# Sinkhorn attention with a gated MLP: q transposed by DMA, head loads begun earlier, natural token order, new order of units

## The chip, the cores and the metric

The kernel runs on one core of a Trainium2 chip. The metric is the device time of one execution in microseconds (us). The kernel before took 166.08 us (median of 3 runs, 165.85 to 168.16). A run more than 1.5% above the fastest of its kernel is called slow.

PE is the matmul engine and PEld its weight loads; DVE, ACT and POOL are the vector, scalar and general engines; SP issues most of the transfers (DMA). PSUM is the memory that matmuls write. A hole is idle time of PE, a landing is the time from the issue of a transfer to its arrival, and the granted clock is the share of PE's full clock that it was given in a stretch (1.00 is full, 0.50 is half).

## The reference, cut to what matters

```python
# q, k, v: [4 batches, 8 heads, 768 tokens, 64]; sort_net: [4, 8, 8, 8]
P = sinkhorn(sort_net)                      # 5 rounds of exp, row and column division
k_sorted = einsum('bhij,bhjcd->bhicd', P, k_blocks)    # 8 blocks of 96 tokens are mixed
v_sorted = einsum('bhij,bhjcd->bhicd', P, v_blocks)
attn = softmax(q_blocks @ k_sorted.T / 8)   # inside each block
x = (attn @ v_sorted), heads side by side   # [4, 768, 512]

h = relu(x @ w_in); u, v = halves of h      # [4, 768, 512] each
v_n = (v - mean) / sqrt(var + 1e-6)
v_s = einsum('ts,bsd->btd', w_spatial, v_n) + b_spatial
out = (u * v_s) @ w_out
```

## The kernel before

One batch is attention, then gated MLP. The program is software-pipelined: while the MLP of batch b runs, attention of batch b+1 is woven into it by a hand-written list of units. A unit is one letter (k: mix and transpose k; q: transpose q; v: mix v; s: score; a: attend; d: divide; V, N, U, S, O: the MLP), an index, a batch, the engine that empties PSUM (A or D), and a PSUM tile (0 to 3).

```python
def load_heads(x, b, name):                       # fp32 in DRAM -> bf16, 768 KB
    t = ld.tile([128, H, G * D], BF16, ...)       # two buffers of each of q, k, v
    nc.gpsimd.dma_start(out=t, in_=...)           # issued from POOL's queue

def vmix(self, hp, eng, ps):                      # mixed v -> vm, then by way of DRAM to vb
    ...
        nc.sync.dma_start(out=vd, in_=self.vm[:, half]...)      # SP's queue
        nc.sync.dma_start(out=self.vb[:, :, half]..., in_=vd...)

def qtr(self, n, eng, ps):                        # 24 transposes on PE, one copy out of PSUM
    for x in range(2):
        for g in range(G):
            for hh in range(2):
                nc.tensor.transpose(t[...], q_in[self.b][...], ident_bf)
    copy(eng, qT, t[:, :, 0:S])

def divide(self, n, eng, ps):                     # xt = acc * exp(-ln(sum))
    nc.vector.tensor_mul(
        out=self.xt[hp].rearrange("p (g i t) -> p i g t", ...)[:, i0:i0 + NB // 2],
        in0=t[:, 0, 0:HW].rearrange("p (i g t) -> p i g t", ...),
        in1=lns.rearrange("p (i g t) -> p i g t", ...))

# in the loop over the list, at the first spatial unit of batch b:
if not gmlp[b].gt and b + 2 < B:                  # the gate
    for x in range(2):
        nc.gpsimd.tensor_copy(out=gate[:, x:x + 1], in_=attn[b + 1].vb[0:1, 0, x, 0, 0:1])
    v_in[b + 2] = load_heads(v, b + 2, "v_in")    # and q_in, k_in
# ... cut ...
```

The gate is two one-element copies on POOL. They read vb, so POOL issues the loads of batch b+2 only after both halves of vb of batch b+1 have landed.

The softmax here doesn't subtract the row's maximum and nothing guards it: scores larger than these inputs give would overflow.

## Time and profile before

| | before |
|---|---|
| median of the runs | 166.11 us |
| profiled run | 169.51 us (slow), span 167.7 us |
| PE / ACT / DVE / POOL busy | 91% / 66% / 58% / 26% |
| mean granted PE clock | 0.968 |
| stage of batch 2, first v projection to the next | 37.8 us |
| stage of batch 3 | 33.7 us |

The prediction below shows the page, the stretches and the PE holes. One view that it only tells is POOL's timeline of the kernel before, around the gate in the stage of batch 2. The columns are start, length, engine, line and instruction, and in brackets the idle time before it and what ended it.

```profile
81.03 0.18 POOL L537 COPY gate<-vb 1x1 bf16<-1x1 bf16 x1 [18.67 <-DMA vb<-vd]
85.78 0.18 POOL L537 COPY gate<-vb 1x1 bf16<-1x1 bf16 x1 [4.57 <-DMA vb<-vd]
86.30 0.94 POOL L93 DMA_DIRECT2D v_in<-in_v_dram  x1 [0.35 <-issue]
...
88.99 4.86 POOL L455 TENSOR_TENSOR gt<-vs,u_sb 128x768 bf16<-128x768 f32 x3
```

POOL stands at the gate until vb has landed, then issues loads, and three multiplications of the MLP have queued up behind.

### The profile page before, as it was taken

Reading aid. Unit: us, or ns where it says so; the run is one execution under the profiler, and the core shown is the slowest. Engines: PE = TensorE matmul, PEld = TensorE weight load, DVE = VectorE, ACT = ScalarE, POOL = GpSimd, SP = SyncE. Lnnn points to the kernel's source line nnn. Section 1 sums busy time; section 2 is a strip of 40 time slices with the busy share of each in tenths; the row PEclk is TensorE's granted clock in tenths of the full one; section 3 lists DMA queues with packets and bytes.
Section 4 is the critical chain, followed back from the end, with each engine's and each line's share of the span. In section 5 each row is a group of like instructions: output and inputs, shape, how many; then the busy total and the mean of one; then the engine's idle time right before and its main releaser. Section 6 shows DMA issues by size and latency. Waiting matters only on the chain.

```text
span 167.7 us, 3907 instructions
## 1 busy us (share of the span) xinstructions
PE 151.9 (91%) x1636; PEld 88.6 (53%) x1645; DVE 97.4 (58%) x203; ACT 110.0 (66%) x181; POOL 43.1 (26%) x46
## 2 busy tenths in 40 slices
PE   0989986999999999999994999999999999999780
PEld 0266853556855544457662454457665544556330
DVE  4667887158971562389222265789232658849951
ACT  3167997459877777689954586489959974560041
POOL 7931000970029550000049330000063300000000
PEclk9999997599999999999999699999999999999999
DMA  2999999999647997604329993605400036000045
GB/s 15 197 204 209 232 257 187 205 203 236 217 110 96 203 204 193 250 33 151 129 72 160 204 195 131 250 31 178 151 23 0 4 131 250 0 0 4 0 182 193
DMA packets 21554, 23.86 MB, mean 142 GB/s; under 512 B 736, under 2 KB 18144, under 8 KB 21408
## 3 DMA queue, kind: packets, MB, share of 16 engines
q0 software_dynamic: 13760, 12.58, 46.8%
q1 hardware_dynamic: 7776, 11.02, 18.3%
q8 instruction: 13, 0.21, 0.5%
q14 instruction: 5, 0.04, 0.1%
HBM read 27.14 MB, written 8.65 MB: 213 GB/s over the span
## 4 chain that ended last, share of the span: by engine, by line
PE 62%; DVE 11%; ACT 10%; DMA 6%; issue 6%; POOL 2%; DVEq 0%; POOLq 0%; SPq 0%; ACTq 0%
PE ps L393 13%; PE ps L443 13%; PE ps L465 10%; PE ps L428 9%; PE ps L352 4%; ACT ex L338 3%; DVE vs L454 3%; PE ps L331 3%; DMA vb<-vd 3%; PE ps L359 2%; DVE gt L455 2%; PE ps L288 2%; PE ps L246 2%; PE ps L276 2%; PE ps L212 2%
## 5 line engine op out<-in xcount | busy, mean ns | idle before, releaser
L443 PE MATMUL ps<-wspT,v_sb 128*128 128x384 bf16 x192 | 34.6, 334 | 0.0
L338 ACT ACTIVATE ex<-ps 96x768 bf16<-96x768 f32 x32 | 24.3, 806 | 8.4 <-PE ps L331 8.3
L454 DVE TENSOR_TENSOR vs<-ps,b_bc 128x768 f32<-128x768 f32 (+1 forms) x20 | 15.9, 794 | 23.7 <-PE ps L443 18.8
L375 DVE TENSOR_TENSOR xt<-ps,lns 128x384 bf16<-128x384 f32 x32 | 16.9, 554 | 19.9 <-ACT lns L371 19.9
L455 POOL TENSOR_TENSOR gt<-vs,u_sb 128x768 bf16<-128x768 f32 x12 | 19.7, 1651 | 34.1 <-ACT ex L338 31.3
L443 PEld LDWEIGHTS <-v_sb 128*128 128x128 bf16 x192 | 18.2, 100 | 12.6 <-issue 1.6
L393 PE MATMUL ps<-w_in_sb,xt 128*128 128x512 bf16 x94 | 24.1, 406 | 0.3 <-DVE xt L375 0.2
L465 PE MATMUL ps<-w_out_sb,gt 128*128 128x512 bf16 x90 | 21.9, 380 | 1.1 <-DVE gt L455 0.8
L407 DVE BATCH_NORM_STATS2 stats<-v_sb 128x6 f32<-128x512 bf16 x24 | 16.3, 677 | 11.0 <-ACT v_sb L227 10.9
L428 PE MATMUL ps<-xt,w_in_sb 128*128 128x384 bf16 x128 | 22.6, 326 | 0.0
L227 ACT ACTIVATE v_sb<-ps 128x1024 bf16<-128x1024 f32 (+1 forms) x15 | 12.5, 852 | 15.5 <-PE ps L393 15.5
L365 ACT ACTIVATE lns<-ps 128x384 f32<-128x384 f32 x32 | 14.5, 486 | 3.9 <-PE ps L359 3.8
L428 PEld LDWEIGHTS <-w_in_sb 128*128 128x128 bf16 x128 | 12.2, 98 | 8.1
L221 ACT COPY o_sb<-ps 128x256 f32<-128x256 f32 (+1 forms) x11 | 7.3, 663 | 13.8 <-DVE o_sb L223 12.1
L393 PEld LDWEIGHTS <-xt 128*128 128x128 bf16 x96 | 9.9, 104 | 12.1 <-issue 2.1
L371 ACT ACTIVATE lns<-lns 128x384 f32<-128x384 f32 x32 | 15.7, 525 | 0.2
L465 PEld LDWEIGHTS <-gt 128*128 128x128 bf16 x96 | 8.6, 98 | 12.4 <-DVE gt L455 1.3
L352 PE MATMUL ps<-ex,vb 96*64 96x96 bf16 x256 | 11.4, 210 | 3.4 <-DVE vs L454 2.5
L352 PEld LDWEIGHTS <-vb 96*64 96x64 bf16 x256 | 8.7, 109 | 8.5 <-issue 7.1
L227 ACT ACTIVATE u_sb<-ps 128x768 bf16<-128x768 f32 x13 | 10.3, 808 | 1.7 <-PE ps L428 1.2
L359 PE MATMUL ps<-ex,ones 96*64 96x384 bf16 x64 | 11.1, 332 | 0.0
L221 ACT CAST kT<-ps 128x768 bf16<-128x768 f32 x13 | 10.0, 806 | 1.1 <-PE ps L288 1.1
(73 smaller groups left out, 177.8 us busy)
## 6 DMA issues: line engine op xcount, KB each, us to landing
out_dram<-o_sb SPq DMA_DIRECT2D x9, 512.0 KB, 2.8
q_in<-in_q_dram POOLq DMA_DIRECT2D x4, 768.0 KB, 10.4
k_in<-in_k_dram POOLq DMA_DIRECT2D x4, 768.0 KB, 13.4
v_in<-in_v_dram POOLq DMA_DIRECT2D x4, 768.0 KB, 9.7
vd<-vm SPq DMA_DIRECT2D x6, 384.0 KB, 3.7
vb<-vd SPq DMA_DIRECT2D x6, 384.0 KB, 3.9
out_dram<-o_sb SPq DMA_DIRECT2D x6, 256.0 KB, 2.1
wsp_nat<-in_moe_w_spatial_dram POOLq DMA_DIRECT2D x1, 1152.0 KB, 21.9
```

Of the source, the lines that this page charges most:

```text
L221: nc.scalar.copy(out=out, in_=in_)
L227: nc.scalar.activation(out=out, in_=in_, func=AF.Relu)
L338: nc.scalar.activation(out=e.rearrange("p h i c -> p h (i c)"), in_=t[0:BLK, :, 0:NB // 2 * BLK], func=AF.Exp, scale=scale,)
L352: nc.tensor.matmul(t[hh * 64:hh * 64 + 64, 0, ii * BLK:(ii + 1) * BLK], lhsT=self.vb[:, i, h // (H // 2), h % (H // 2), :], rhs=self.e[n][ ...
L375: nc.vector.tensor_mul(out=self.xt[hp].rearrange("p (g i t) -> p i g t", g=G, i=NB)[:, i0:i0 + NB // 2], in0=t[:, 0, 0:HW].rearrange("p (i ...
L393: nc.tensor.matmul(t[:, x, :], lhsT=self.xt[kc][:, g * 128:(g + 1) * 128], rhs=w_in_sb[:, kc, DH:DFF], start=(kc == 0), stop=(kc == KC - 1),)
L407: nc.vector.bn_stats(out=stats, in_=v_sb[:, x, :])
L428: nc.tensor.matmul(t[:, x, 0:HW], lhsT=w_in_sb[:, kc, mc * 128:(mc + 1) * 128], rhs=self.xt[kc][:, x * HW:(x + 1) * HW], start=(kc == 0), ...
L443: nc.tensor.matmul(t[:, x, 0:HW], lhsT=self.v[g][:, mc * 128:(mc + 1) * 128], rhs=wspT[:, g, x * HW:(x + 1) * HW], start=(g == 0), stop=(g ...
L454: nc.vector.tensor_add(out=vs[:, x], in0=t[:, x, 0:HW], in1=b2[:, x])
L455: eng.tensor_mul(out=gt2[:, x], in0=vs[:, x], in1=u2[:, x])
L465: nc.tensor.matmul(t[:, x, :], lhsT=self.gt[mc][:, g * 128:(g + 1) * 128], rhs=w_out_sb[:, mc, :], start=(mc == 0), stop=(mc == FC - 1),)
```

## The change

The intent: take the q transposes of batches 1 to 3 off PE (which is full), issue the loads earlier so that POOL is not held at the gate, and let the first v projection start before the last divides. The core of the diff:

```diff
-    wsp_nat ... moe_w_spatial.rearrange("(p g) s -> p g s", g=G)
+    wsp_nat ... moe_w_spatial.rearrange("(g p) s -> p g s", p=128)      # natural token order
...
+        def qdma(self, n, eng, ps):
+            qr = qr_pool.tile([128, G, H, D], BF16, name="qr", tag="qr")
+            nc.vector.tensor_copy(out=qr..., in_=q_in[self.b]...)
+            nc.sync.dma_start(out=self.q_tile(), in_=qr..., transpose=True)
...
+            if self.b == 0:          # attend of batch 0: extra matmuls for the PE clock
+                for _ in range(2):
+                    for hh in range(2):
+                        nc.tensor.matmul(t[hh * 64:hh * 64 + 64, 1, HW:512], lhsT=ones, ...)
...
-                out=self.xt[hp].rearrange("p (g i t) -> p i g t", ...)[:, i0:i0 + NB // 2],
-                in0=t[:, 0, 0:HW].rearrange("p (i g t) -> p i g t", ...),
+                out=self.xt[hp][:, ih * HW:(ih + 1) * HW].rearrange("p (i t g) -> p i t g", ...),
+                in0=t[:, 0, 0:HW].rearrange("p (i g t) -> p i t g", ...),   # and in1 alike
...
+        load_batch(2)                # before the list of units begins
...
                 if b not in gmlp:
                     gmlp[b] = Gmlp(b)
+                    if 0 < b < B - 2:
+                        load_batch(b + 2)
-                    if not gmlp[b].gt and b + 2 < B:
-                        gate = ...   # gate and loads behind it: gone
-                    eng = DVE if b == B - 1 else nc.gpsimd
+                    eng = DVE if b == B - 1 and len(gmlp[b].gt) == FC - 1 else nc.gpsimd
```

Cut: the shorter way from p to the mixing matrices, the order of the first loads, buffer counts, the whole new list of units.

## The prediction

> **What bounds the kernel now.** I read the page first (engine shares, slices, chain), then the busy table by stretches, the timeline of PE with its idle notes, the waits, the landings of the first loads, and the timelines of ACT, DVE and POOL.
>
> ```profile
> PE 151.9 (91%) x1636; PEld 88.6 (53%) x1645; DVE 97.4 (58%) x203; ACT 110.0 (66%) x181; POOL 43.1 (26%) x46
> ...
> PEclk9999997599999999999999699999999999999999
> ...
> PE 62%; DVE 11%; ACT 10%; DMA 6%; issue 6%; POOL 2%; DVEq 0%; POOLq 0%; SPq 0%; ACTq 0%
> ```
>
> PE is busy 91% and is 62% of the chain that ended last, but the clock row has two dips, one after 25 us and one after 92 us. By stretches (us, busy per engine, granted clock):
>
> ```profile
> 13.20:28.10 14.90, 12.79 (x282) 9.61 (x281) 11.66 (x18) 14.30 (x27) 0.20 (x1) 0.97 1.12 224
> 28.10:46.50 18.40, 18.18 (x195) 11.65 (x196) 11.76 (x23) 11.82 (x17) 7.48 (x4) 0.84 1.13 213
> 46.50:67.00 20.50, 20.42 (x219) 11.15 (x218) 9.71 (x19) 15.64 (x27) 9.90 (x9) 1.00 0.93 162
> 67.00:104.80 37.80, 35.16 (x375) 20.24 (x376) 17.70 (x34) 27.61 (x43) 9.55 (x9) 0.95 0.66 147
> 104.80:138.50 33.70, 33.57 (x375) 19.48 (x376) 19.06 (x35) 26.38 (x42) 6.56 (x4) 1.00 0.27 96
> ```
>
> After window and length the columns are PE, PEld, DVE, ACT, POOL, clock, DMA share and GB/s. Batch 0's attention (13.2 to 28.1) is bound by ACT, 14.3 of 14.9 us. From 28 us PE is full, so PE work taken out there comes off one for one. The stretches from 67.0 and from 104.8 hold the same work (375 matmuls each), but the first is 4.1 us longer. Finer stretches show the lost clock:
>
> ```profile
> 24.00:28.00 4.00, 2.18 (x45) 1.19 (x39) 2.72 (x7) 4.00 (x11) 0.00 (x0) 0.91 1.02 199
> 28.00:32.00 4.00, 3.78 (x13) 1.67 (x14) 1.07 (x3) 0.40 (x2) 2.84 (x2) 0.50 1.30 202
> 32.00:36.00 4.00, 4.00 (x27) 2.43 (x25) 1.64 (x4) 2.79 (x4) 4.00 (x3) 0.73 1.32 204
> ...
> 92.00:96.00 4.00, 4.00 (x34) 2.17 (x28) 1.02 (x2) 2.49 (x5) 1.85 (x2) 0.57 1.32 204
> ```
>
> Lost clock is 4 x (1 - granted): 0.36 + 2.0 + 1.08 = **3.4 us** around 24 to 36, and 1.7 us at 92. PE's timeline has these lines:
>
> ```profile
> 91.72 0.36 PE L352 MATMUL ps<-ex,vb 96*64 96x96 bf16 x8 [2.46 <-DVE vs L454]
> 115.47 0.84 PE L276 MATMUL ps<-ident_bf,q_in 128*64 128x128 bf16 x24
> 158.75 4.06 PE L465 MATMUL ps<-w_out_sb,gt 128*128 128x512 bf16 x18 [0.81 <-DVE gt L455]
> ```
>
> The first is a hole of 2.46 us. POOL's timeline explains it: POOL waited at the gate copies until both halves of vb had landed (85.78), issued three loads (86.3 to 89.0), and only then multiplied three gated tiles (4.86 us), so the PSUM tiles behind them came free late. Hole and cold clock (2.46 + 1.7) are the 4.1 us above. The profiled run took 169.51 us and is marked slow; the median is 166.08. So I count the hole in a fast run as much smaller. The second line is a q transpose unit; the third the wait in the tail.
>
> **What the Trainium skill says.** "TensorE: Matmul & The Clock Gate", Part 1: the PE clock is half or full, and about one idle window of 3.4 us drops it to half. The trace agrees: 0.50 granted from 28 to 32, after a stretch with PE busy only 2.18 of 4 us. "VectorE: DVE Perf Modes", The three transpose paths: a 128x128 bf16 transpose takes 390 ns on TensorE and 1309 ns by DMA. In this trace 24 half-width ones take 0.67 us on the chain, 28 ns each when pipelined. "DMA: Bandwidth & Descriptors", Latency and other measured facts: a DMA transpose moves an effective 261 GB/s; no run here shows one. "VectorE: DVE Perf Modes", the perf-mode tier table: a bf16 SBUF copy of 2048 elements takes 693 ns; the trace before has no such copy.
>
> **The change part by part.**
> q by DMA: removes 6 units of 24 transposes, 6 x 0.67 = 4.0 us of PE, 1.34 a batch, all on PE-bound stretches. It also removes their PSUM copies (1444 ns on ACT or 957 ns on DVE), and adds three DVE copies of 3072 elements, about 1 us each by the skill's table (an estimate), and three transposes of 768 KB. At 261 GB/s one takes 786 KB / 261 = 3.0 us plus about 2 us fixed: 5 us. At 1309 ns a block, one after the other, 24 x 1.309 = 31 us. They are issued some 15 to 20 us before the first score, so the first is hidden and the second is not.
>
> Start: transpose and spread of p go from PE-copy-PE-copy to two DVE transposes and one group of matmuls, and pdiag reads PSUM. Between p_bf (11.22) and the first k matmul (13.21) this saves about 0.3 us.
>
> Stage 0 to 1: in natural order the first three token groups need only the even units of attention, so V00 need not wait for the last divides. V now starts at 28.13; with one ACT kT copy less (0.8 us) and two units of slack I put it at 26.8. Extra matmuls in batch 0's attends (column pairs run together: 32 small ones, 16 x 55 ns = 0.9 us in ACT-bound time) and vmix units moved there should hold the clock; that is worth up to the 3.4 us. PE alone then needs, up to the first k unit, three V (5.2), three U (3.9), v11 (0.33) and five w (1.7): 37.9. But the loads were moved too. Before (issue on POOL plus time to landing, from the views of each tile), w_in landed at 21.9, wsp at 28.7, v1 at 32.6, k1 at 36.5, q1 at 40.3, so a head tile takes 3.9 us and wsp 5.5. In the new order: v1 25.8, q1 29.6, wsp 35.1, k1 39.0. So the w units wait about 1.3 us and k starts near 39.4. Adding four k (1.36), w40 (0.33), four scores (0.98) and U10 (1.3), S starts at 43.4. Before, S started at 47.26 with U30 (1.41) and a score (0.25) undone, thus 48.9. Gain **5.5 us**; without waits for loads it would be 7.
>
> Stages 2 and 3: 2 x 1.34 = **2.7 us**. Gate removed and loads issued earlier: I choose **0.7 us** for a fast run.
>
> Tail: now each of four units makes DVE do two adds and two multiplies, 2 x (0.55 + 0.56) = 2.2 us or 8.7 in all, against 2.06 of PE; PE then waits 0.81 us. Afterwards three multiplies go to POOL (1.65 us each, inside the 2 us rhythm) and only the last is split: **0.9 us**.
>
> The strided reads of the divide and the 2 KB instead of 4 KB output rows I count as zero. Sum: 5.5 + 2.7 + 0.7 + 0.9 = 9.8, so 156.3; I give back 1.2 us for new small waits of the new order: **157.5 us**.
>
> **Rivals.** (1) The DMA transpose is slow, or holds up the vd and vb transfers behind it on the same SP queue, and scores or attends wait. For it: the page's 1309 ns per block. Against it: the lead of most of a stage and low DMA load later (share 0.27 to 0.66). At 31 us each of three stages would wait 10 us or more: 185 us or worse. If only vb comes late, 1 to 3 us once: 159 to 160. (2) The clock still drops at the start of stage 1, since batch 0 stays ACT-bound and PE has gaps: then 2 to 3 us are not gained, 160. (3) Loads become the bound in stage 1: the 1.5 us already taken off, perhaps 1.5 more, 159. (4) The hole near 92 was in the median runs too: then 2 to 3 us more are gained, 155.
>
> **Range and chances.** With rival 2 plus a late vb about 162, with rival 4 and all steps right about 153.5. The limit of 2% is 162.8. Faster 0.88, same 0.09, slower 0.03 (the slow transpose).
>
> **What would show it.** No PE transposes of q in batches 1 to 3, and PE's total about 3 us less. Clock of 0.9 or more from 24 to 36. First V matmul before 27.5 and first S near 43.4, with waits for wsp or k_in in front of w or k. A landing time under 15 us for the transpose, and no score that waits for it. No gate and no PE hole of over 1 us in the third stage; the stages of batches 2 and 3 near 32.4 us. No gap before the last output projection. The prediction is wrong if PE shows waits on qT or vb, or if a stretch other than the first load waits stays under 95% PE.

## The result, and the profile after

The changed kernel took **192.25 us** (191.2 to 194.28, 4 runs). It is slower by a factor of 1.157 (95% interval 1.151 to 1.163). A ratio here is the mean time of one kernel's fast runs over that of the other's fast runs of the same rounds, so it is not quite the ratio of the medians. The predicted range was 153.5 to 162.

The page of the changed kernel answers to the first lines of the prediction:

```profile
PE 152.7 (79%) x1529; PEld 86.2 (45%) x1529; DVE 108.1 (56%) x203; ACT 101.0 (52%) x169; POOL 46.9 (24%) x44
...
PEclk9999999999555756999997579999999999999999
...
PE 46%; DMA 39%; DVE 5%; POOL 4%; issue 2%; ACT 2%; POOLq 1%; DVEq 0%
DMA qT<-qr 22%; PE ps L482 13%; PE ps L504 11%; DMA k_in<-in_k_dram 11%; PE ps L466 7%; PE ps L431 6%; DMA vd<-vm 4%; PE ps L361 3%; DVE vs L493 3%; PE ps L389 2%; DMA vb<-vd 2%; PE ps L396 2%; DVE xt L411 2%; POOL v_in L93 1%; POOLq L596 1%
```

DMA's share of the chain that ended last has gone from 6% to 39%, with the transpose of q alone at 22%. The clock row has two long dips. PE's timeline of the changed kernel has these holes:

```profile
43.35 1.20 PE L318 MATMUL ps<-pdiag,k_in 128*64 128x128 bf16 x36 [2.97 <-DMA k_in<-in_k_dram]
...
55.86 0.88 PE L361 MATMUL ps<-qT,kT 64*96 64x96 bf16 x16 [10.41 <-DMA qT<-qr]
...
69.26 0.53 PE L389 MATMUL ps<-ex,vb 96*64 96x96 bf16 x8 [6.08 <-DMA vb<-vd]
...
107.20 0.88 PE L361 MATMUL ps<-qT,kT 64*96 64x96 bf16 x16 [6.62 <-DMA qT<-qr]
```

2.97 + 10.41 + 6.08 + 6.62 = 26.1 us of PE standing still, all behind a DMA. The busy table of the changed kernel shows what follows a hole (after window and length: PE, PEld, DVE, ACT, POOL, granted clock, DMA share, GB/s):

```profile
45.50:55.90 10.40, 0.04 (x2) 0.04 (x3) 2.98 (x8) 0.33 (x2) 0.00 (x0) 0.64 1.31 183
55.90:60.00 4.10, 4.10 (x40) 2.38 (x40) 0.55 (x1) 1.56 (x3) 0.00 (x0) 0.50 1.28 225
```

PE works again from 55.9 us, at half clock. Summing length times (1 - clock) over the working stretches after the three long holes (55.9 to 64, 69.3 to 80, 107.2 to 116) gives 9.2 us. Holes and half clock are 35.3 us. In the profile of the kernel before the same items were 7.6 us (2.46 of hole, 1.7 and 3.4 of half clock). The difference is 27.7; less the 3 us or so of PE work that the change takes away (4.0 of transposes, less 0.9 of extra matmuls) this is about the 24.8 us between the spans (192.5 and 167.7).

SP's timeline of the changed kernel shows what the queue did:

```profile
30.80 14.80 SPq L310 DMA_TRANSPOSE qT<-qr  x1
45.66 0.57 SPq L275 DMA_DIRECT2D vd<-vm  x1
...
90.06 13.20 SPq L310 DMA_TRANSPOSE qT<-qr  x1
...
126.93 3.66 SPq L310 DMA_TRANSPOSE qT<-qr  x1
```

One instruction, three times: it held the SP queue for 14.80, 13.20 and 3.66 us, and landed after 25.0, 17.0 and 5.5 us. The first ran beside the rest of the first loads and the loads of batch 2, the second beside the loads of batch 3 (issued from 83.9 to 86.6 us on POOL), the third beside no load. The first vd, whose source was ready earlier, could be issued only at 45.66 us.

And the divide, one line each from the views of tile xt of the kernel before, of the changed kernel, and of the experiment a4 below (min/median/max in ns):

```profile
L375 DVE TENSOR_TENSOR xt<-ps,lns x32: 544/557/559, 22.5 to 137.4; 128x384 bf16<-128x384 f32 x32
```

```profile
L411 DVE TENSOR_TENSOR xt<-ps,lns x32: 792/806/827, 21.8 to 163.2; 128x384 bf16<-128x384 f32 x32
```

```profile
L411 DVE TENSOR_TENSOR xt<-ps,lns x32: 1427/1472/1622, 21.9 to 154.0; 128x384 bf16<-128x384 f32 x32
```

### The profile page after: what moved, and what is told of

The parts are those of the page before. It is cut to its first block, busy times and chain, and to the rows that moved or that the text cites. A ratio compares the mean times of both kernels' runs of the same rounds, so it can differ in the third digit from the quotient of the medians.

```text
span 192.5 us, 3673 instructions
## 1 busy us (share of the span) xinstructions
PE 152.7 (79%) x1529; PEld 86.2 (45%) x1529; DVE 108.1 (56%) x203; ACT 101.0 (52%) x169; POOL 46.9 (24%) x44
## 2 busy tenths in 40 slices
DMA packets 32657, 26.20 MB, mean 136 GB/s; under 512 B 10048, under 2 KB 28224, under 8 KB 32640
## 3 DMA queue, kind: packets, MB, share of 16 engines
q0 software_dynamic: 14400, 12.58, 42.4%
## 4 chain that ended last, share of the span: by engine, by line
PE 46%; DMA 39%; DVE 5%; POOL 4%; issue 2%; ACT 2%; POOLq 1%; DVEq 0%
DMA qT<-qr 22%; PE ps L482 13%; PE ps L504 11%; DMA k_in<-in_k_dram 11%; PE ps L466 7%; PE ps L431 6%; DMA vd<-vm 4%; PE ps L361 3%; DVE vs L493 3%; PE ps L389 2%; DMA vb<-vd 2%; PE ps L396 2%; DVE xt L411 2%; POOL v_in L93 1%; POOLq L596 1%
## 5 line engine op out<-in xcount | busy, mean ns | idle before, releaser
L494 POOL TENSOR_TENSOR gt<-vs,u_sb 128x768 bf16<-128x768 f32 x15 | 24.7, 1645 | 128.7 <-DVE vs L493 99.0
L482 PE MATMUL ps<-wspT,v_sb 128*128 128x384 bf16 x192 | 36.7, 350 | 0.0
L411 DVE TENSOR_TENSOR xt<-ps,lns 128x384 bf16<-128x384 f32 x32 | 24.7, 806 | 18.1 <-ACT lns L408 18.1
L493 DVE TENSOR_TENSOR vs<-ps,b_bc 128x768 f32<-128x768 f32 (+1 forms) x17 | 15.5, 910 | 29.4 <-PE ps L482 29.4
L361 PE MATMUL ps<-qT,kT 64*96 64x96 bf16 x256 | 11.8, 234 | 18.1 <-DMA qT<-qr 17.0
L482 PEld LDWEIGHTS <-v_sb 128*128 128x128 bf16 x192 | 19.1, 104 | 14.4 <-issue 3.9
L466 PE MATMUL ps<-xt,w_in_sb 128*128 128x384 bf16 x128 | 25.5, 351 | 0.0
L431 PE MATMUL ps<-w_in_sb,xt 128*128 128x512 bf16 x96 | 22.0, 379 | 0.2 <-DVE xt L411 0.2
L361 PEld LDWEIGHTS <-kT 64*96 64x96 bf16 x256 | 9.1, 142 | 24.1 <-issue 12.1
L239 ACT ACTIVATE v_sb<-ps 128x1024 bf16<-128x1024 f32 (+1 forms) x15 | 12.5, 852 | 12.5 <-PE ps L431 12.5
L235 DVE CAST kT<-ps 128x768 bf16<-128x768 f32 x12 | 11.2, 949 | 6.8 <-PE ps L318 6.7
L233 ACT COPY o_sb<-ps 128x256 f32<-128x256 f32 (+1 forms) x10 | 6.3, 629 | 15.6 <-DVE o_sb L235 11.8
L431 PEld LDWEIGHTS <-xt 128*128 128x128 bf16 x96 | 9.4, 98 | 11.2 <-issue 0.5
## 6 DMA issues: line engine op xcount, KB each, us to landing
q_in<-in_q_dram POOLq DMA_DIRECT2D x4, 768.0 KB, 18.8
k_in<-in_k_dram POOLq DMA_DIRECT2D x4, 768.0 KB, 26.8
```

The costliest lines, as they stand in the source:

```text
L361: nc.tensor.matmul(t[0:BLK, hh, ii * BLK:(ii + 1) * BLK], lhsT=self.k[hp][rows, i * BLK:(i + 1) * BLK], rhs=self.q[rows, hp, i], start=Tru ...
L411: nc.vector.tensor_mul(out=self.xt[hp][:, ih * HW:(ih + 1) * HW].rearrange("p (i t g) -> p i t g", t=TB, g=G,), in0=t[:, 0, 0:HW].rearrang ...
L431: nc.tensor.matmul(t[:, x, :], lhsT=self.xt[kc][:, g * 128:(g + 1) * 128], rhs=w_in_sb[:, kc, DH:DFF], start=(kc == 0), stop=(kc == KC - 1),)
L466: nc.tensor.matmul(t[:, x, 0:HW], lhsT=w_in_sb[:, kc, mc * 128:(mc + 1) * 128], rhs=self.xt[kc][:, x * HW:(x + 1) * HW], start=(kc == 0), ...
L482: nc.tensor.matmul(t[:, x, 0:HW], lhsT=self.v[g][:, mc * 128:(mc + 1) * 128], rhs=wspT[:, g, x * HW:(x + 1) * HW], start=(g == 0), stop=(g ...
L493: nc.vector.tensor_add(out=vs[:, x], in0=t[:, x, 0:HW], in1=b2[:, x])
```

## The experiments

Two theories. **A**: the DMA transpose is slow and everything else follows. **B**: transfers that run at the same time slow each other, and the early head loads are the root: they slow the transpose, and vd and vb as well. Rivals for parts: the SP queue order, the strided divide, the new order of units. All 15 runs gave the right output. The a-series ran on one chip, the c-series on another, the d- and e-series on a third; ratios are to runs of the kernel before. The medians below are of all runs, slow ones too.

| run | what it is | median us | ratio to before |
|---|---|---|---|
| changed | | 192.25 | 1.157 |
| a1_q_pe | changed, q on PE | 176.98 | 1.055 |
| a2_gate | changed, loads behind the landed transpose | 192.17 | 1.148 |
| a3_vq | changed, vd and vb on POOL's queue | 204.21 | 1.213 |
| a4_q_pe_div | a1, divide reads in order, writes strided | 185.33 | 1.104 |
| c1_vbgate | changed, loads behind vb | 172.50 | 1.034 |
| c2_q_pe_vbgate | a1, loads behind vb | 167.45 | 1.002 |
| c3_perm | c2, token order of before | 167.43 | 0.995 |
| c4_q23_dma | c3, q of batches 2, 3 by DMA | 164.41 | 0.972 |
| d2_wout_late | c4, output weights loaded behind vb | 161.18 | 0.970 |
| d1_nofill | d2, no extra matmuls in attend | 160.31 | 0.965 |
| d3_before_q23 | before, q of batches 2, 3 by DMA | 167.81 | 1.010 |
| d4_nat | d2, natural token order | 162.95 | 0.981 |
| e1_load3_early | d1, loads of batch 3 early | 171.53 | 1.030 |
| e3_best_q_pe | d1, all q on PE | 164.37 | 0.991 |
| e2_before_again | before | 167.45 | 1.005 |

### a1_q_pe: q on PE again

```diff
-  ... a70-1 d70-- q01A- v01A3 ...          (and q02, q03)
+  ... k31A0 r01D1 k01D3 r11D2 k21A0 ...    (r: the unit qtr of before; banks shifted)
```

> The changed kernel with one part undone: q of batches 1 to 3 transposed on PE again (six units of 24 transposes put back, PSUM banks shifted, all else kept). Theory 'the DMA transpose is the loss': the two holes before the scores (10.4 and 6.6 us), the hole before attend that waits for vb (6.1) and about 9 us of half clock after them go, 4.0 us of PE comes back: about 160 to 162 us. Rival 'the new order, the early loads or the strided divide cost it': stays above 172 us, with holes of other causes.

Measured 176.98 us, a miss: 15 us came back, not 31. The PE timeline of a1 has a new largest hole, and the chain of a1 tells its cause:

```profile
57.39 0.53 PE L389 MATMUL ps<-ex,vb 96*64 96x96 bf16 x8 [7.80 <-DMA vb<-vd]
```

```profile
37.03 11.29 DMA vd<-vm
48.34 9.00 DMA vb<-vd
```

With no transpose anywhere, vd took 11.29 us and vb 9.00 us in the stage of batch 1. In the kernel before, the longest were 4.7 and 4.6 us. What runs beside them are the loads of batch 2, issued from 20.4 to 27.1 us, and the rest of the first loads: c4 below, where the loads of batch 2 are held, still has 9.3 and 8.5 us at most. Theory A alone is dead.

### a2_gate: loads behind the landed transpose

```diff
-        load_batch(2)
+                if name == "q" and b in (1, 2):
+                    nc.gpsimd.tensor_copy(out=gate[:, 0:1], in_=attn[b].qT[0:1, 0, 0:1])
+                    load_batch(b + 1)
```

> The changed kernel, but the loads of batch b+2 are issued only after the DMA transpose of q of batch b+1 has landed (a one-element copy on POOL reads the transposed tile). Theory 'the transpose is slow only beside head loads': the second transpose lands in about 5.5 us instead of 17 and its hole of 6.6 us goes; the first still runs beside the rest of the first loads, lands in about 15 us instead of 25; total 172 to 178. Rival 'the transpose is slow by itself, and the fast third one is an exception': landing times stay 25 and 17 and the total stays near 192.

The transposes did land sooner, after 16.0, 5.9 and 5.5 us. Yet the total did not move: 192.17 us, where 172 to 178 was expected, a miss. PE's timeline of a2 shows where the time went:

```profile
65.98 0.53 PE L389 MATMUL ps<-ex,vb 96*64 96x96 bf16 x8 [9.40 <-DMA vb<-vd]
...
111.92 0.53 PE L389 MATMUL ps<-ex,vb 96*64 96x96 bf16 x8 [7.60 <-DMA vb<-vd]
```

The loads now fell onto vd and vb, whose longest landings were 12.1 us each; in front of the first scores 4.38 us of waiting for the transpose was left. One wait was traded for the other, which is what theory B says and theory A does not.

### a3_vq: vd and vb on another queue

```diff
-                nc.sync.dma_start(out=vd, ...)        # and vb
+                nc.gpsimd.dma_start(out=vd, ...)      # and vb
```

> The changed kernel with the transfers vd and vb issued from POOL's queue instead of SP's, so that they need not wait for the issue of the transpose. Theory 'the queue order holds vb back': first vd issued near 34 us instead of 45.7, the hole of 6.1 us before attend of batch 1 goes, total 6 to 9 us less, about 184. Rival 'the DMA engines are full and vb comes late from any queue': hole stays, total within 2 us of 192.

204.21 us, worse by 12, and the hole before attend of batch 1 grew to 11.52 us. The view of tile vd of a3 says:

```profile
DMA to landing us min/median/max: 2.7/4.8/30.1
```

A vd now landed 30.1 us after its issue. POOL's queue also carries the head loads, and vd came behind them. So this run does not tell how much of the 6.1 us hole was SP's queue order. It shows only that sharing a queue with the loads is worse than sharing one with the transpose.

### a4_q_pe_div: the other side of the stride

```diff
-   out= ... "p (i t g) -> p i t g",  in0, in1 = ... "p (i g t) -> p i t g"   # reads strided
+   out= ... "p (i t g) -> p i g t",  in0, in1 = ... "p (i g t) -> p i g t"   # write strided
```

> As a1_q_pe, but the divide reads PSUM and the logs in order and writes its bf16 output with a stride of 12 bytes, instead of reading both fp32 inputs with a stride of 64 bytes. Theory 'the strided fp32 reads cost 806 instead of 554 ns': the divide is back near 554 ns, DVE busy falls by about 8 us, the first V matmul starts 1 to 2 us earlier, total 2 to 3 us under a1_q_pe. Rival 'any stride costs it, or DVE is off the path': 800 ns again, or the total within 0.5 us of a1_q_pe.

The opposite: 1472 ns a divide, as shown above, and 185.33 us, 8.3 us over a1. Natural order needs a stride on one side, and reading fp32 at 64 bytes (804 ns in a1) is far cheaper than writing bf16 at 12 bytes (1472 ns). In the order of the kernel before neither is needed: it reads and writes runs of 16 tokens.

### c1_vbgate and c2_q_pe_vbgate: the gate of the kernel before

```diff
-        load_batch(2)
-                    if 0 < b < B - 2:
-                        load_batch(b + 2)
+                    if not gmlp[b].gt and b + 2 < B:       # at the first spatial unit
+                        ... two copies of attn[b + 1].vb on POOL ...
+                        load_batch(b + 2)
```

> The changed kernel with one part undone: the loads of batch b+2 are held, as in the kernel before, until both halves of vb of batch b+1 have landed (two one-element copies on POOL at the first spatial unit). q stays by DMA. Theory 'transfers slow each other: early loads delay the transpose, vd and vb': second transpose lands in about 5.5 us, its hole (6.6) and half clock go; vb of batch 1 comes some 4 us after its issue; the first transpose still runs beside the rest of the first loads, 15 to 25 us. Total 172 to 178. Rival 'the transpose itself holds vb back through the SP queue': vb holes of 6 us or more stay, total above 184.

172.50 us with q still by DMA. The transposes landed after 18.8, 5.9 and 6.8 us: only the first, beside the first loads, is slow, and it leaves a hole of 5.19 us. Behind it vb leaves one of 2.71 us, after which the clock stayed full:

```profile
59.17 0.36 PE L389 MATMUL ps<-ex,vb 96*64 96x96 bf16 x8 [2.71 <-DMA vb<-vd]
```

```profile
56.00:60.00 4.00, 1.29 (x25) 0.67 (x25) 0.96 (x1) 0.27 (x1) 0.61 (x3) 1.00 0.40 98
60.00:64.00 4.00, 3.92 (x44) 2.44 (x43) 2.40 (x3) 3.50 (x7) 4.00 (x5) 1.00 0.77 90
```

> As a1_q_pe (q on PE), with the loads held behind vb as well. Theory 'what a1 still lost was vb delayed by early loads': its hole of 7.8 us before attend of batch 1, the 0.8 us one and about 2 us of half clock go: 165 to 168 us, level with the kernel before. Rival 'order of units and strided divide cost as much': above 171.

167.45 us, level with the kernel before. The hole before attend of batch 1 did not go: in the profiled run, a slow one, 2.64 us are left, with half clock after it. The view of tile vd of c2 says:

```profile
DMA to landing us min/median/max: 2.3/4.4/9.6
```

c4 below, profiled in a fast run, has 9.3 us. The new order issues the first vd at 30 to 31 us, beside the first loads; the kernel before issued it at 39.5. So the gate alone does not make vd quick. Together with the changed kernel and a1 this is a table of two by two (median us):

| | loads early | loads behind vb | difference |
|---|---|---|---|
| q by DMA | 192.25 | 172.50 | 19.8 |
| q on PE | 176.98 | 167.45 | 9.5 |
| difference | 15.3 | 5.1 | |

The early loads cost more than the transpose does, and each is worse with the other. (By the fast runs alone the differences are 19.3 and 9.6, 15.0 and 5.3. The columns are from different chips; the ratios 1.157, 1.055, 1.034 and 1.002 say the same.)

### c3_perm and c4_q23_dma: token order, and the transpose where it is alone

```diff
 c3: divide, w_spatial view, bias copy and output view as in the kernel before
 c4: r12, r02, r13, r03 out of the list, q02A- and q03A- back in (batch 1 stays on PE)
```

> As c2_q_pe_vbgate, with the token order of the kernel before (divide, spatial weights, bias and output view), the new order of units kept. Theory 'the strided reads of the divide cost DVE 32 x 0.25 = 8 us, of which some lies on the path': divide back at 554 ns, total 1 to 3 us under c2. Rival 'natural order pays by letting the first v projection start before the last divides': total 1 us or more above c2.

167.43 against 167.45 us: no difference by the medians, but the c3 runs fall into two groups (166 and 169 us). The fast runs alone, two of c3 and three of c2, are 1.2 us apart in favour of the old order. This is too few to conclude; d4 repeats it.

> As c3_perm, but q of batches 2 and 3 by DMA again, where no load now runs beside them; batch 1 stays on PE. Theory 'the transpose is good where it has the DMA engines for itself': both land in about 5.5 us, no score waits, 4 x 0.67 = 2.7 us of PE goes, total 2 to 3 us under c3. Rival 'it costs elsewhere (SP queue, output stores, vd)': same as c3 or above.

164.41 us, 3.0 under c3 by the medians (3.7 by the two fast runs of each), and the first version ahead of the kernel before, with both transposes landing after 5.8 and 6.5 us. But its runs too fall into 162.2, 162.5 and 166.3, 166.4 us. In the profiled run, a fast one, the hole before the first attend of batch 1 was 1.44 us long and the clock stayed at 1.00. In c3 that hole was 3.03 us and the clock from 52 to 56 us was 0.65.

### d2_wout_late: fewer first loads ahead of vb

```diff
-    nc.gpsimd.dma_start(out=w_out_sb, ...)          # among the first loads
+                        if b == 0:
+                            nc.gpsimd.dma_start(out=w_out_sb, ...)   # behind the gate
                         load_batch(b + 2)
```

> As c4_q23_dma, with the load of the output weights (512 KB, first read after 60 us) moved from the first loads to behind vb of batch 1. Theory 'the first loads fill the DMA engines until about 43 us, so vd and vb of batch 1 come late, and the hole in front of its attend, with half clock after it when it is long, makes c4 fall into two groups (162 and 166 us)': hole under 1 us, no half clock near 52 to 56, all runs near 160 to 162. Rival 'the two groups have another cause': median stays at 164 with both groups.

161.18 us, six runs between 161.0 and 161.29. The hole before that attend is gone and so is the second group; the longest landings of vd and vb went from 9.3 and 8.5 us (c4) to 7.4 and 6.8. 512 KB that nobody needed before 60 us had stood beside them. c4 ran on another chip and none of its slow runs was profiled, so that this hole made the second group is argued. For it: d1, d4 and e3, with the same edit, have no such hole, and all their runs lie within 1%.

### d1_nofill: without the extra matmuls

```diff
-            if self.b == 0:
-                for _ in range(2): ... warm matmuls ...
```

> As d2_wout_late, without the extra matmuls in the attends of batch 0. Theory 'they hold the PE clock': granted clock from 24 to 36 us falls to 0.7 to 0.9, 1 to 3 us slower than d2. Rival 'natural density of the new order holds it alone': clock 1.00 there and the time within 0.5 us of d2, or less by up to 0.9 us.

160.31 us, 0.9 faster: the rival was right. The busy table of d1 around the end of batch 0's attention:

```profile
24.00:28.00 4.00, 2.60 (x45) 1.42 (x45) 3.39 (x6) 3.94 (x10) 0.00 (x0) 1.00 1.32 204
28.00:32.00 4.00, 4.00 (x20) 1.66 (x19) 2.28 (x5) 2.11 (x3) 0.00 (x0) 1.00 1.16 235
```

The clock is 1.00 with PE busy 2.60 of 4 us; the kernel before had 2.18 of 4 us there and 0.50 in the next stretch. The new order, with v units moved in, held the clock in this run without the extra matmuls. This is the best version: 3.5% under the kernel before.

### d3_before_q23: the DMA transpose alone in the kernel before

```diff
-  ... k12A0 q12D3 k02A1 q02A2 ...          (and batch 3)
+  ... O00A3 Q02A- V01-1 ... k12A0 k02A3 ...
```

> The kernel before with one part of the change alone: q of batches 2 and 3 by DMA (issued before the first v projection of the batch before, after the head loads have landed), q of batches 0 and 1 on PE, its own order of units and load gate. Theory 'the DMA transpose gains its 2.7 us wherever no loads run beside it': landing 5.5 to 7 us, 2.5 to 3 us under the kernel before. Rival 'in that order it delays vd and vb or the stores': no gain.

A miss: 167.81 us, 1% slower, though both transposes landed after 6.2 and 6.6 us. Stage by stage, from one first v projection to the next, d3 took 38.3 and 32.6 us in batches 2 and 3, where the kernel before (e2 below) took 37.4 and 33.7. In batch 3 PE's saving arrives. In batch 2 PE only comes sooner to the hole in front of attend, which is 2.79 us instead of 2.06, and the clock after it is 0.65 and 0.50 instead of 0.85 and 0.72. That hole comes from POOL behind the gate, which the transposes do not touch. These two profiles add up to the same (165.7 and 166.3 us), because the profiled run of e2, at 168.1 us, was a long one. The 1% shows in the mean clocks of the runs: 0.961 to 0.971 in all six of d3, 0.981 to 0.998 in the fast runs of the kernel before. The averages differ by 0.027, and 0.027 of 166 us is 4.5 us of lost clock (an estimate), more than the 2.7 us gained. Why every run of d3 loses so much clock is not shown.

### d4_nat: natural token order in a good kernel

```diff
 d2 with the changed kernel's divide, w_spatial view, bias load and output view
```

> As d2_wout_late, but with the natural token order of the changed kernel (strided divide at 804 ns, first v projection after the even units only). Theory 'natural order costs on the whole: DVE 8 us more, of which holes of 0.34 us three times and a first v projection that starts 0.9 us later are on the path': 1 to 2 us slower than d2. Rival 'no difference, as c2 and c3 showed': within 0.5 us.

162.95 against 161.18 us in the same rounds: natural order costs 1.8 us. The first v projection started at 29.56 us, not earlier but 0.9 us later than in d2 (28.64), where DVE was busy 3.48 of 4 us from 24 to 28; here it was full (3.99), and PE waited 0.23 us for the last divide. d4 changes the token order as a whole, so the 1.8 us are not the divide's alone.

### e1_load3_early: one edit back

```diff
                     gmlp[b] = Gmlp(b)
+                    if b == 1:
+                        load_batch(3)
-                        load_batch(b + 2)            # behind the gate: for batch 2 only
+                        if b == 0:
+                            load_batch(b + 2)
```

> As d1_nofill, with one edit: the three head loads of batch 3 are issued when the gmlp of batch 1 starts, as in the changed kernel, and not behind vb of batch 2. Theory 'head loads beside the transpose and beside vd and vb make both late': transpose of batch 2 lands in 13 to 17 us instead of 6.5, scores or attends of batch 2 wait 5 us or more, half clock after it, total 168 to 174. Rival 'the first-load phase alone was the trouble': within 2 us of d1 (160.3).

171.53 us, 11.2 over d1 (10.8 by the fast runs) from moving one call. PE's timeline of e1, and SP's timeline of d1 and then of e1:

```profile
86.20 0.88 PE L361 MATMUL ps<-qT,kT 64*96 64x96 bf16 x16 [8.88 <-DMA qT<-qr]
```

```profile
66.34 4.87 SPq L310 DMA_TRANSPOSE qT<-qr  x1
```

```profile
66.31 12.82 SPq L310 DMA_TRANSPOSE qT<-qr  x1
```

The transpose held SP's queue for 12.82 us and landed after 19.8 us, where d1 had 4.87 and 6.8 at most. The clock from 80 to 92 us was 0.55, 0.50 and 0.67. vd was issued at 79.8 us, 7 us later than in d1, just after the transpose let go of the queue. The loads, issued from 60.6 to 63.3 us, are the only edit: theory B is shown here.

### e3_best_q_pe: what the transpose is worth

```diff
 d1 with q02A-, q03A- out, units qtr of batches 2 and 3 back in
```

> As d1_nofill, with q of batches 2 and 3 on PE again. Theory 'a transpose that has the DMA engines to itself takes its 4 x 0.67 = 2.7 us off PE and costs nothing': 163 us, 2.7 us over d1. Rival 'it also costs (DVE copy, SP queue)': less than 1.5 us over d1.

164.37 us, 4.1 over d1. First v projections of batches 1 and 2 in PE's timeline, d1 and then e3:

```profile
65.01 1.89 PE L423 MATMUL ps<-w_in_sb,xt 128*128 128x512 bf16 x8
...
97.52 1.89 PE L423 MATMUL ps<-w_in_sb,xt 128*128 128x512 bf16 x8
```

```profile
64.76 1.89 PE L423 MATMUL ps<-w_in_sb,xt 128*128 128x512 bf16 x8
...
99.22 1.89 PE L423 MATMUL ps<-w_in_sb,xt 128*128 128x512 bf16 x8
```

32.51 against 34.46 us, and the same again for the next stage (97.52 to 130.03, 99.22 to 133.67): 1.95 us a batch. Of it 1.34 are PE's transposes and 0.49 is a hole in e3 before the first score of the batch, which waits for ACT's copy of kT; 0.1 is left over.

### e2_before_again: a fast profile of the kernel before

> The kernel before, unchanged, for a profile of a fast run and for the spread. If the hole before attend near 92 us is in a fast run as well, removing the gate was worth more than the 0.7 us of the prediction, and the half clock after it is what tells fast from slow; if not, the prediction's reading stands. Time within 0.5% of 166.

Its profiled run counts as fast, span 166.3 us, and the hole is in it:

```profile
90.27 0.36 PE L352 MATMUL ps<-ex,vb 96*64 96x96 bf16 x8 [2.06 <-DVE vs L454]
```

```profile
88.00:92.00 4.00, 1.94 (x31) 1.24 (x30) 0.96 (x1) 2.11 (x5) 4.00 (x3) 0.85 1.31 202
92.00:96.00 4.00, 4.00 (x40) 2.20 (x39) 1.85 (x3) 1.96 (x4) 0.41 (x1) 0.72 1.32 204
```

2.06 us and then (0.15 + 0.28) x 4 = 1.7 us of half clock. The four runs went from 165.97 to 168.85 us (median 0.9% above 166, so the expected 0.5% was missed). The profiled one took 168.1 us at a clock of 0.978, 1.3% above the fastest, just inside the rule for fast. The fastest runs of this kernel in the three calls (164.97 to 165.85 us) had clocks of 0.997 to 1.000, hence next to no half clock anywhere; whether they had the hole, no profile shows.

## Why the prediction was wrong, point by point

Two steps failed, and the table of two by two has their sizes. "Gate removed and loads issued earlier", booked as a gain of 0.7 us, cost 19.8 us with the transposes and 9.5 without. "So the first is hidden", of a transpose of 5 us, failed with it: the transpose was not hidden, and cost 15.3 us beside the early loads and 5.1 with the gate. Both fail for one reason, shown by a1, c1, c2 and e1: transfers that run together delay each other.

**The size of the DMA transpose, and its rival 1.** The prediction had two sizes, 5 us (bytes over 261 GB/s plus a fixed part) and 31 us (24 blocks one after the other), and put its weight on the first. As a transfer by itself 5 us was nearly right: 5.5 to 7.0 us wherever no load ran. (Its "about 2 us fixed" names no source; stores of 256 and 512 KB in the kernel before landed after 2.1 and 2.8 us, which as an estimate leaves 1.4 us.) It wrote against the rival "low DMA load later (share 0.27 to 0.66)", and that is the faulty line. The share was read from the trace of the kernel before. The same change moves the loads to where the transposes are, and the first one runs inside the first loads in any case. Beside loads it took 16.0 to 25.0 us. The load to ask for is that of the changed kernel at that moment, and the diff had it. Rival 1's "185 us or worse" came near the 192.25 by luck: its mechanism, 31 us in each of three stages, did not occur, and the third transpose landed after 5.5 us with no wait.

**What the gate is worth.** The prediction booked its removal as a gain of 0.7 us. The gate looked like idle POOL time; in the kernel before, together with a late issue of vd, it kept vd and vb at 4.7 us or less (5.5 in e2). The prediction saw vd and vb at risk only from the SP queue, not from the loads.

**The hole in a fast run.** "I count the hole in a fast run as much smaller" is not borne out: e2, fast by the rule, has 2.06 and 1.7 us. But its run was a long one, so rival 4 is shown for one fast run and open for the fastest. The new order of units with the gate (d1) has no such hole: from 64 to 98 us PE was busy 33.96 of 34.0 us.

**The strided divide counted as zero.** It measured 806 instead of 557 ns, 8.0 us of DVE in 32 divides; natural token order as a whole cost 1.8 us (d4 against d2). The first v projection did not start at 26.8 but at 29.1 us. The divide has only a part in that: with the old divide and token order it started at 28.7 (d1).

**Loads in stage 1.** wsp landed at 35.9 us, where 35.1 was predicted, and no w unit waited the 1.3 us. Predicted landing of k of batch 1: 39.0 us. Without a transpose beside it: 40.4 (d1), and with early loads before 41.1 (a1). Beside a transpose: 42.7 without early loads (c1), 43.3 with them (changed), and PE waited 2.97 us for it. The first spatial unit (S) was predicted at 43.4 us. It started at 60.15, and even in d1 at 46.84. That is 2.1 us before the 48.9 from which the prediction counted, so d1 has 2.1 of the 5.5 us (its q of batch 1, back on PE, takes 1.34). Its gain lies elsewhere: up to the first v projection of batch 1 d1 is 0.8 us ahead of e2 (65.01 against 65.83), in the stages of batches 2 and 3 it is 4.9 and 1.2 us ahead, and in the tail 0.9. As e2 was a long run, these are high values.

**The clock at the start of stage 1.** Right as a fact: 1.00 from 24 to 36 us, against 0.91, 0.50 and 0.73. Wrong in the cause: d1 holds it without the extra matmuls. Their cost was right (0.9 us, and d1 is 0.9 under d2). The 3.4 us at stake were those of a slow run: e2 has 1.00, 0.67 and 0.90 there, 1.7 us. "The trace agrees" holds for the half clock only: from 24 to 28 us PE was idle 1.8 us in all, not for 3.4 us at once. The gain was spent waiting for transfers in the changed kernel.

**PE time saved by q.** Right in mechanism, too small in size: 1.95 instead of 1.34 us a batch where it can be seen alone (d1 against e3), because a wait for a copy goes with it. The DVE copy that the transfer needs took 0.95 us, as estimated. The stages of batches 2 and 3 were predicted near 32.4 us; d1 has 32.51 twice, the changed kernel 42.4 and 33.3.

**The tail.** Right: no gap before the last output projection, and from the last first v projection to the end 28.6 instead of 29.4 us, 0.8 where 0.9 was predicted. (The prediction's 8.7 us of DVE should be 8.9; nothing hangs on it.)

**Why small packets lose** was argued, not shown. The Trainium skill, "DMA: Bandwidth & Descriptors", Queues, rings and completion order, says that an engine takes turns between its queues packet by packet. The profiles show only sizes: the changed kernel has 9312 more packets under 512 B than the kernel before (10048 against 736), 3104 a transpose, so about 253 B each, against 12.58 MB / 14400 = 874 B in the loads' queue. Whether a packet of the profile is what the page calls a packet, which holds several descriptors (the single pieces of a transfer), is not shown. A transpose that alternates with three head loads would be done about when they are: 5.5 + 3 x 3.9 = 17 us as an estimate, with 17.0 and 19.8 measured (16.0 to 25.0 in all). No run changed the packet size, so it stays open. How much of the 6.1 us wait for vb was SP's queue order stays open too (a3). With the loads held, the wait for vb was 2.71 us behind a transpose that held the queue for 12.82 us (c1) and 2.64 without one (c2), but in c1 PE had waited 5.19 us for the transpose first.

## What to carry to other kernels

A transfer is hidden only against the traffic of the new kernel: list what else the DMA engines carry at that moment, with the transfers on the short path (here vd, vb and the transpose) first, and hold bulk loads behind them. A wait that looks like idle time on a side engine may be a traffic light; before taking it out, ask what would then run at the same time. Take a bundle of changes apart: here the transpose is worth 4 us in the new order of units with no load beside it (e3 against d1) and nothing in the old order (d3), later output weights remove a hole, while early loads, natural order and extra matmuls each cost.

## What the Trainium skill lacked or had wrong

- "VectorE: DVE Perf Modes", The three transpose paths: 1309 ns for a 128x128 block by DMA. Here 24 blocks landed in 5.5 to 7.0 us, 0.23 to 0.29 us a block, so the figure cannot be multiplied.
- "DMA: Bandwidth & Descriptors", Latency and other measured facts: 261 GB/s for a transpose with a non-contiguous middle dimension. Here, alone, 786 KB in 5.5 us to landing are 143 GB/s; they are 225 with the prediction's 2 us of fixed time taken off (an estimate), so the rate must not be used without a fixed part. I found no time there for a transpose beside loads: 16.0 to 25.0 us here.
- No page says that loads lengthen the time for which the issue of a DMA transpose holds its queue: 3.5 to 5.2 us alone, 12.5 to 14.8 us beside loads. The only figures that I found are cycles per number of tiles, given for comparison with trn3.
- "VectorE: DVE Perf Modes", the tier table: a two-tensor operation with a PSUM operand has one tier, and strides are not in the table (the skill speaks of them on other pages, without a time for such an operation). Here the same 128x384 multiplication took 557 ns, 806 ns with both fp32 inputs read at 64 bytes, and 1472 ns with its bf16 output written at 12 bytes.
- "TensorE: Matmul & The Clock Gate", Part 1: about one idle window of 3.4 us drops the clock. Here half clock followed a hole of 2.06 us (e2), but not one of 1.44 us (c4) nor one of 2.71 us (c1), so the length of one hole does not tell.
